# One core, block-sparse attention and a two-layer FFN: the same operations and transfers in another stored order, with 17 instead of 14 matmuls on zeros ahead of the first keys

## The chip, the cores and the metric

The kernel runs on one core of one Trainium2 chip. The engines named below are TensorE (PE), VectorE (DVE), ScalarE (ACT), GpSimd (POOL) and SyncE (SP, which here only issues transfers). The metric is the device time of one execution in microseconds. Before the change it is 259.52 us, the median of three runs (258.18 to 260.66).

## The reference

Inputs are q, k and v of 4 batches, 8 heads, 768 tokens and 64 columns, and the weights w_in (512 x 2048) and w_out (2048 x 512). Each head's keys are cut into 12 blocks of 64. A query attends to its own block and to the three blocks with the best gate scores, causally:

```python
k_rep = k.reshape(B, H, n_blocks, block, D).mean(axis=3)
gate_scores = np.einsum('bhsd,bhnd->bhsn', q, k_rep)
gate_scores = np.where(causal, gate_scores, -1000000000.0)
top_idx = np.argsort(gate_scores, axis=-1)[..., -top_k:]
...
scores = scale * np.matmul(q, k.transpose(0, 1, 3, 2))
mask = mask & (pos[:, None] >= pos[None, :])
scores = np.where(mask, scores, -1000000000.0)
attn = softmax(scores)
out = np.matmul(attn, v)
...
x = out.transpose(0, 2, 1, 3).reshape(B * S, H * D)
h = x @ w_in
g = 0.5 * h * (1.0 + np.tanh(c * (h + 0.044715 * h * h * h)))
return (g @ w_out).astype(np.float32)
```

(The softmax is written out in the reference; it is shortened here.) The 3072 tokens are the four batches one after the other, so the FFN of one batch needs all eight heads of that batch and nothing of the next.

## The kernel before

The work is cut into 16 pairs of heads, four pairs to a batch. A pair of the first batch goes through these steps, each on the engine named.

- SP (and for part of pair 0 ACT's queue) loads q, k and v of the pair (L392, L426). PE transposes q and k in float32, three 128 x 128 tiles at a time (`turn`, L548); ACT and DVE copy the results out (L361, L365).
- DVE sums the keys of each block (`ksb_h`, L583 and L589), PE multiplies q with these sums (the gate, L687), and DVE turns the result into a mask: a transpose (L703), the causal gate (L710), the eight largest of twelve (L719), and two steps that make the additive mask (L720, L724). PE transposes the mask (L756).
- PE computes the scores with the mask as part of the contraction (`st_e`, L863), ACT the exponentials (L882), POOL the causal triangle (an affine_select, L908). POOL also casts v (L363). PE multiplies with v (L931), DVE divides by the row sums (L949, L950), and PE transposes the output (L988).

The later batches have the same steps at other lines: q and k are transposed on DVE (L564) and cast (`kc_all`, `q16`: L363 on POOL, L361 on ACT or L365 on DVE), scores at L1046, exponentials at L1059, triangle at L1073, the product with v at L1085, the division at L969.

The FFN of a batch follows its attention and is interleaved with the attention of the next batch. `s1` (L1122) is x times w_in with the gelu on ACT (L1134). The second product of the first batch is plain (`s2_plain`, L1322). The later batches use a Strassen-like scheme with seven products instead of eight: `w_sums` (L1291) prepares sums of w_out on DVE, `sums` (L1309) sums of the activations on DVE, L1372 are the products, and the joins (L1421) add the parts on DVE. The last batch does a part of the first product in the same manner (L1170, L1211, L1235). Stores are issued at L1456 and L1465.

The weights are loaded by POOL (`load_w`): a small copy (L456) that waits for an earlier transfer, and then two transfers of a half each (L460). For w_in the copy waits for v of pair 2. SP has a transfer of its own that reads w_in (L1567) and waits until w_in is there; the loads of pair 4 (k, then q, then v) stand behind it on SP's queue. For w_out the copy waits for q of pair 4. So the order of the transfers is w_in, then k and q of pair 4, then w_out.

`warm` adds matmuls on zeros (L1524, 128 x 128 weights, 256 columns; "fillers" below). They depend on nothing and nothing reads them; each is executed where the order has it.

The order of everything is stored. All operations are first collected in a list with their numbers; `ORDER` gives the order in which they are emitted, `BUFFER` which buffer of a group each operation takes, and `ENGINE` which of the possible engines does an operation that more than one can do:

```python
for n in ORDER:
    op = self.ops[n]
    for kind, key in op.takes:
        if key not in self.buf:
            self.buf[key] = self.kinds[kind][0][next(picks)]
    op.emit(engine.get(n, next(iter(op.engines))))
```

Each engine works its own operations off in this order, and waits for others by semaphores. So of the one stored order only the order on each engine, and on each queue, is seen on the chip. Numbers that the text below speaks of: 71 and 62, 66 are the first transposes of pair 0 (q; k's first and second half), 75 its first gate, 157 the load of w_in, 172 that of w_out, 236 an affine_select of pair 1, 393 the first matmul of the FFN, 1890 to 1961 the fillers.

Of the kernel before, what the change touches and what calls it, by code (L numbers as in the profile page):

```python
# [21 lines left out]
    0, 22, 1890, 1891, 9, 1892, 1893, 1894, 6, 2, 1895, 1896, 1897, 1898,  # L22
    1899, 1900, 1901, 1, 1902, 12, 1903, 71, 1904, 15, 23, 1905, 1906, 1907,
    1908, 1909, 3, 1910, 72, 18, 1911, 62, 1912, 5, 1913, 82, 19, 1914, 195,
    1915, 31, 66, 64, 68, 73, 63, 74, 1916, 75, 1917, 100, 1918, 76, 1919,
    1920, 78, 77, 32, 67, 101, 35, 1921, 84, 93, 85, 89, 194, 83, 200, 79,
    4, 36, 80, 44, 1922, 1923, 98, 94, 1924, 196, 1925, 99, 1926, 201, 95,
    86, 91, 1927, 87, 113, 102, 90, 214, 114, 215, 103, 205, 104, 1928, 118,
    120, 202, 219, 26, 197, 206, 27, 119, 1929, 106, 210, 45, 52, 39, 115,
    40, 109, 107, 53, 121, 30, 111, 48, 1930, 1931, 129, 49, 220, 130, 198,  # L30
    203, 1932, 105, 207, 211, 122, 234, 131, 110, 249, 208, 123, 216, 235,
    1933, 1934, 57, 125, 133, 58, 250, 124, 240, 212, 224, 217, 221, 241,
    1935, 43, 157, 126, 127, 153, 134, 229, 254, 236, 222, 140, 225, 255,
    1936, 1937, 141, 138, 230, 242, 245, 155, 151, 231, 268, 238, 243, 149,
    232, 246, 237, 139, 269, 145, 1938, 279, 135, 142, 251, 263, 1939, 258,
    247, 1940, 280, 252, 264, 143, 270, 56, 1941, 144, 274, 283, 256, 275,
    259, 1942, 1943, 163, 1944, 284, 146, 276, 272, 147, 164, 226, 277, 285,
    288, 289, 227, 313, 281, 1945, 61, 297, 314, 165, 286, 1946, 302, 265,
    266, 290, 298, 271, 299, 308, 292, 168, 260, 303, 169, 300, 304, 309,
    293, 1947, 317, 322, 305, 310, 294, 306, 311, 261, 323, 315, 326, 318,  # L40
    393, 295, 328, 394, 329, 356, 395, 363, 1948, 396, 364, 1949, 319, 320,
    397, 365, 366, 324, 172, 367, 403, 404, 405, 178, 406, 358, 359, 327,
    360, 179, 330, 407, 361, 428, 429, 430, 335, 1950, 331, 362, 431, 336,
    339, 418, 419, 341, 432, 420, 421, 182, 398, 399, 1951, 400, 422, 401,
    408, 409, 410, 411, 402, 388, 183, 412, 389, 342, 390, 186, 391, 352,
    353, 392, 354, 355, 338, 383, 384, 385, 386, 343, 357, 344, 337, 413,
    387, 414, 415, 187, 347, 631, 349, 433, 416, 368, 434, 435, 369, 370,
    417, 346, 584, 1952, 436, 585, 373, 437, 371, 374, 345, 372, 632, 375,
    438, 376, 587, 378, 377, 439, 588, 379, 380, 348, 423, 440, 441, 442,
    424, 425, 426, 381, 443, 586, 444, 445, 427, 446, 447, 382, 448, 553,  # L50
    451, 635, 452, 453, 454, 449, 455, 574, 456, 457, 458, 575, 590, 459,
    460, 461, 566, 462, 567, 636, 1953, 463, 557, 464, 465, 466, 558, 470,
    552, 471, 472, 595, 473, 474, 475, 554, 476, 570, 190, 568, 477, 334,
    467, 591, 478, 692, 592, 571, 593, 555, 1954, 594, 479, 576, 1955, 693,
    191, 561, 480, 644, 559, 645, 481, 482, 483, 484, 572, 647, 485, 488,
    569, 696, 596, 489, 573, 562, 490, 486, 598, 491, 577, 697, 648, 622,
    556, 597, 560, 623, 563, 614, 639, 650, 578, 615, 492, 493, 564, 651,
    652, 654, 609, 640, 610, 494, 653, 495, 624, 957, 958, 601, 602, 496,
    497, 498, 605, 499, 705, 606, 655, 500, 656, 618, 658, 565, 646, 611,
    706, 603, 583, 501, 502, 709, 1956, 619, 616, 503, 507, 607, 657, 961,  # L60
    674, 508, 620, 711, 1957, 617, 682, 621, 625, 626, 509, 504, 510, 643,
    604, 511, 608, 512, 612, 683, 675, 665, 666, 712, 715, 678, 613, 713,
    513, 514, 627, 679, 700, 708, 628, 661, 716, 707, 515, 516, 714, 676,
    669, 677, 579, 517, 970, 518, 717, 662, 663, 580, 519, 670, 520, 667,
    664, 718, 521, 668, 680, 962, 719, 701, 726, 971, 974, 684, 671, 722,
    727, 681, 1020, 976, 704, 522, 672, 685, 1021, 728, 525, 686, 723, 739,
    526, 527, 735, 977, 673, 1024, 740, 528, 730, 741, 736, 529, 1025, 978,
    1958, 724, 737, 530, 1148, 731, 531, 743, 725, 468, 732, 729, 1033,
    1034, 532, 744, 733, 1037, 687, 738, 742, 533, 745, 756, 534, 980, 746,
    734, 840, 1039, 535, 747, 536, 981, 979, 1144, 758, 1040, 537, 748, 841,  # L70
    749, 972, 538, 450, 759, 1086, 1041, 1042, 544, 1145, 760, 761, 973,
    539, 545, 762, 540, 842, 1959, 843, 1082, 546, 768, 844, 769, 770, 1157,
    771, 1036, 1083, 830, 772, 1035, 831, 832, 833, 752, 1160, 1158, 1087,
    753, 754, 834, 755, 757, 1149, 763, 764, 765, 1095, 766, 825, 1096, 541,
    505, 1099, 767, 826, 548, 1101, 827, 773, 982, 828, 1161, 829, 782, 783,
    1045, 784, 1473, 523, 785, 792, 793, 786, 547, 794, 795, 835, 836, 837,
    1098, 1163, 1410, 796, 838, 774, 839, 811, 812, 984, 813, 814, 1102,
    1164, 787, 788, 1044, 789, 542, 815, 790, 777, 1043, 791, 845, 778, 779,
    780, 801, 487, 1028, 781, 1103, 802, 1104, 803, 804, 806, 985, 805, 807,
    808, 549, 809, 965, 816, 1165, 797, 817, 1105, 798, 818, 819, 810, 849,  # L80
    850, 851, 820, 1960, 1006, 852, 989, 966, 853, 1166, 846, 821, 775, 997,
    1048, 969, 854, 1414, 822, 855, 856, 857, 1535, 1007, 859, 860, 998,
    858, 861, 1097, 1029, 1477, 799, 823, 862, 1107, 863, 1002, 864, 865,
    1411, 847, 1090, 1008, 550, 1478, 1003, 1032, 993, 999, 866, 868, 1047,
    988, 1152, 994, 551, 990, 1004, 869, 870, 1010, 1005, 995, 1153, 800,
    1011, 871, 776, 1169, 991, 867, 872, 824, 1159, 1064, 1065, 1536, 1009,
    873, 1055, 1056, 874, 992, 996, 1059, 1060, 1000, 875, 1072, 877, 1073,
    878, 879, 1109, 848, 1012, 1068, 876, 1066, 1069, 1013, 1113, 880, 1001,
    885, 1014, 1114, 1156, 886, 887, 881, 888, 1110, 1423, 1070, 1106, 1067,
    1091, 1074, 524, 1474, 1051, 1415, 1015, 1071, 1075, 889, 890, 891, 892,  # L90
    895, 1061, 1418, 1052, 1115, 896, 1053, 1117, 897, 1118, 893, 1167, 898,
    1054, 1539, 894, 882, 899, 900, 901, 1492, 1076, 902, 1171, 904, 1597,
    1119, 1601, 1168, 905, 1172, 1094, 1121, 906, 907, 1130, 903, 908, 909,
# [1533 lines left out]
```

## Time and profile before

| what | value |
|---|---|
| times of the runs | 258.18, 259.52, 260.66 us |
| the profiled execution's own time | 259.66 us |
| its span, and what lies around it | 257.9 us, 1.76 us |
| PE busy | 249.0 us, 97% |
| DVE busy | 193.0 us, 75% |
| ACT busy | 180.6 us, 70% |
| POOL busy | 85.8 us, 33% |
| fillers (L1524) | 72 |
| TensorE clock shown as granted | 1.00 throughout |

In the rows of the profile, "L1122 PE MATMUL wide<-xT,w_in" is line 1122 on PE, writing the tile `wide` from `xT` and `w_in`. In the timeline the first two numbers are start and duration in microseconds, rows of one kind are merged ("x14"), and what ended the engine's idle time before stands in brackets. In the chain of waits the numbers are start and duration too. In the table by stretches come, after the stretch and its length, the busy time of PE, of PE's weight loads, of DVE, ACT and POOL (engines without work are left out), the granted clock, the share of the transfer engines and GB/s. In lists of waits come the total, the number and the longest, in microseconds.

### The profile page before, as it was taken

The page shows a single profiled execution, that of the slowest core. Times are in us where ns is not written, and L with a number is a line of the kernel's source. Part 1 is how long each engine was busy: PE and PEld are TensorE (multiplying, and loading weights), DVE is VectorE, ACT ScalarE, POOL GpSimd, SP SyncE. Part 2 cuts the span into 40 slices and gives each one's busy share as a digit, 9 for nine tenths or more (in the row PEclk, how much of TensorE's full clock was granted, in tenths as well). Part 3 has the DMA queues.
Part 4 walks back from the last instruction along what each step waited for, and adds up shares of the span by engine and source line. Part 5 has one row for each costly group of instructions (what it writes and reads, how often), then busy time and mean ns, then how long its engine had stood idle before and what let it go on. Part 6 is the DMA issues. An engine that isn't in the chain of part 4 may idle for free.

```text
span 257.9 us, 6488 instructions
## 1 busy us (share of the span) xinstructions
PE 249.0 (97%) x2506; PEld 172.8 (67%) x2506; DVE 193.0 (75%) x537; ACT 180.6 (70%) x228; POOL 85.8 (33%) x167
## 2 busy tenths in 40 slices
PE   6999999999999999999998999999999999999994
PEld 4767777655556665665776888556778787666883
DVE  1698955345248999998999987999797765678843
ACT  2487897655889999677987787566899857558200
POOL 8557551401045746120382445001184610000000
PEclk9999999999999999999999999999999999999999
DMA  7999969999999996999959948329131340120024
GB/s 151 221 220 169 218 114 145 145 185 179 145 146 139 134 151 133 140 204 193 140 107 177 198 117 137 64 44 265 25 56 47 61 82 34 41 84 0 4 81 163
DMA packets 130927, 32.62 MB, mean 126 GB/s; under 512 B 124528, under 2 KB 126928, under 8 KB 130896
## 3 DMA queue, kind: packets, MB, share of 16 engines
q1 hardware_dynamic: 126160, 27.62, 59.3%
q0 software_dynamic: 3136, 4.19, 10.0%
q10 hardware_dynamic: 1600, 0.39, 0.8%
q8 instruction: 19, 0.31, 0.5%
q14 instruction: 12, 0.10, 0.1%
HBM read 27.26 MB, written 6.29 MB: 130 GB/s over the span
## 4 chain that ended last, share of the span: by engine, by line
PE 80%; DVE 13%; ACT 2%; DMA 2%; issue 1%; POOL 0%; ACTq 0%; DVEq 0%
PE wide L1122 24%; PE bank L1372 18%; PE wide L1046 9%; PE bank L1322 8%; PE bank L1085 5%; PE wide L1211 5%; DVE XS L1309 2%; PE wide L863 2%; DVE sel L719 2%; PE bank L687 2%; PE bank L1524 2%; PE bank L931 2%; DMA G<-in_q_dram 2%; DVE sel L710 1%; PE bank L548 1%; PE bank L988 1%
## 5 line engine op out<-in xcount | busy, mean ns | idle before, releaser
L1122 PE MATMUL wide<-xT,w_in 128*128 128x384 f16 x416 | 73.7, 326 | 0.0
L1059 ACT ACTIVATE ats<-wide 128x896 f16<-128x896 f32 x72 | 63.6, 916 | 9.2 <-PE wide L1046 6.8
L1134 ACT ACTIVATE G<-wide 128x768 f16<-128x768 f32 x52 | 42.0, 809 | 25.6 <-PE wide L1122 25.5
L1122 PEld LDWEIGHTS <-w_in 128*128 128x128 f16 x416 | 39.8, 98 | 25.3 <-issue 1.0
L1073 POOL TENSOR_SCALAR_AFFINE_SELECT ats<-ats 128x256 f16<-128x256 f16 x72 | 32.0, 457 | 54.0 <-ACT ats L1059 50.0
L1046 PE MATMUL wide<-qT,kT 76*128 76x512 f16 (+3 forms) x192 | 38.9, 305 | 0.0
L1372 PE MATMUL bank<-w_out,G 128*128 128x256 f16 x216 | 32.2, 272 | 0.9 <-DVE osb L1421 0.9
L1372 PEld LDWEIGHTS <-G 128*128 128x128 f16 x288 | 27.0, 97 | 7.6 <-issue 1.2
L1322 PE MATMUL bank<-w_out,G 128*128 128x512 f16 x96 | 28.1, 379 | 0.0
L1421 DVE TENSOR_TENSOR osb<-bank,osb 128x512 f32<-128x512 f32 (+1 forms) x38 | 22.3, 594 | 7.2 <-PE bank L1372 4.4
L1085 PEld LDWEIGHTS <-ats 128*128 128x128 f16 x504 | 22.6, 98 | 5.8 <-POOL ats L1073 1.0
L564 DVE STREAM_TRANSPOSE s<-sd 128x768 f32<-128x768 f32 x24 | 23.1, 968 | 3.8 <-DMA sd<-in_q_dram 3.4
L1085 PE MATMUL bank<-v,ats 128*128 128x65 f16 x504 | 24.7, 194 | 0.3 <-POOL ats L1073 0.3
L882 ACT ACTIVATE ats<-wide 128x1024 f16<-128x1024 f32 (+3 forms) x24 | 20.9, 918 | 4.5 <-PE wide L863 4.3
L1046 PEld LDWEIGHTS <-kT 76*128 76x128 f16 x192 | 17.3, 98 | 10.0 <-issue 0.5
L363 POOL CAST kT<-s 64x768 f16<-64x768 f32 x20 | 17.3, 865 | 20.1 <-DVE s L564 19.7
L1372 PEld LDWEIGHTS <-XS 128*128 128x128 f16 x216 | 19.8, 98 | 4.5 <-DVE XS L1309 0.4
L1372 PE MATMUL bank<-TS,XS 128*128 128x256 f16 x144 | 22.6, 272 | 0.1
L363 POOL CAST v<-vsd 128x768 f16<-128x768 f32 x13 | 11.3, 870 | 26.9 <-DMA vsd<-in_v_dram 26.9
L1524 PE MATMUL bank<-XS 128*128 128x256 f16 x72 | 17.1, 326 | 1.1 <-DVE ks L302 1.1
L703 DVE STREAM_TRANSPOSE sel<-bank 128x160 f32<-128x160 f32 (+2 forms) x17 | 5.5, 330 | 14.7 <-PE bank L687 14.5
L969 DVE TENSOR_TENSOR xn<-bank,zr 128x384 f16<-128x384 f32 x24 | 13.4, 557 | 0.8
(116 smaller groups left out, 373.8 us busy)
## 6 DMA issues: line engine op xcount, KB each, us to landing
out_dram<-osb SPq DMA_DIRECT2D x23, 256.0 KB
vsd<-in_v_dram SPq DMA_DIRECT2D x26, 192.0 KB
sd<-in_k_dram SPq DMA_DIRECT2D x48, 96.0 KB
sd<-in_q_dram SPq DMA_DIRECT2D x48, 96.0 KB
w_in<-in_moe_w_in_dram POOLq DMA_DIRECT2D x2, 1024.0 KB, 11.3
w_out<-in_moe_w_out_dram POOLq DMA_DIRECT2D x2, 1024.0 KB, 12.8
G<-in_k_dram SPq DMA_DIRECT2D x6, 192.0 KB
TS<-in_v_dram SPq DMA_DIRECT2D x6, 192.0 KB
```

Of the source, the lines that this page charges most:

```text
L363: nc.gpsimd.tensor_copy(out=out, in_=in_)
L564: nc.vector.transpose(out=T[key + "T32", p], in_=T[key, p].rearrange("p t j -> p (t j)"))
L1046: nc.tensor.matmul(st[:, x:e], kT16[i][h][0:76, s0:s0 + 128], qT16[i][h][0:76, s0 + (x - cb):s0 + (e - cb)], start=True, stop=True)
L1059: nc.scalar.activation(out=T["at", u][:, 0:n], in_=plan.buf[("st",) + u][:, 0:n], func=AF.Exp, bias=0.0, scale=SCALE)
L1073: nc.gpsimd.affine_select(out=dg, in_=dg, compare_op=ALU.is_ge, fill=0.0, base=0, pattern=[[0, 2], [1, 128]], channel_multiplier=-1)
L1085: nc.tensor.matmul(pvv[:, qc, 0:65], at[:, cb + (qc - jc) * 128: cb + (qc - jc + 1) * 128], v16[i][:, jc, h, :], start=(gi == 0 and jc == ...
L1122: nc.tensor.matmul(hps[:, 512 * e:512 * e + HALF], w_in16[:, ci, (2 * j + e) * 128: (2 * j + e + 1) * 128], T["xT", b][:, ci, HALF * h:HAL ...
L1134: nc.scalar.activation(out=G[:, :, h, j, :], in_=plan.buf["hps", b, j, h].rearrange("p (e w) -> p e w", e=2)[:, :, 0:HALF], func=AF.Gelu_a ...
L1322: nc.tensor.matmul(plan.buf["ops", b, ti], G[:, f % 2, 2 * ti // NC, f // 2, ti % (NC // 2) * 128:ti % (NC // 2) * 128 + 128], w_out16[:, ...
L1372: nc.tensor.matmul(dst[:, HD * h:HD * h + HD], FACT[m][0][:, j, t * 128:(t + 1) * 128], FACT[m][1][:, j, :], start=(clear and j == 0), sto ...
L1421: nc.vector.tensor_tensor(out=dst(), in0=src(), in1=other(), op=ALU.add)
L1524: nc.tensor.matmul(plan.buf["warm", n][:, 0:256], zero16, z, start=True, stop=True)
```

## The change

The three tables are replaced; no other line changes. Operations and transfers are the same but for one filler that is left out (71 instead of 72). What is different on each engine:

- **PE**: 17 fillers stand ahead of the first transposes (operation 71) instead of 14, then 4 instead of 8 ahead of the next (62), 2 instead of 4 ahead of the third (66), and 2 instead of 1 between the fourth (73) and the first gate (75). Ahead of the first matmul of the FFN (393) stand 63 fillers instead of 58, behind it 8 instead of 14. The other matmuls are permuted locally.
- **POOL**: the load of w_in (157) comes behind the affine_select 236 instead of ahead of it, and ahead of a cast of v instead of behind it. A cast of k of pair 4 (337) comes ahead of w_out's load (172). The constants at the start are in another order.
- **SP**: the first ten transfers are the same; then v of pair 0 comes ahead of k of pair 3, and fills and some pairs of transfers change places.
- **DVE** and **ACT**: local permutations. Eleven operations go to DVE (nine from ACT, two from POOL) and eleven leave it (eight to ACT, three to POOL).

```diff
 ORDER = [
-    0, 22, 1890, 1891, 9, 1892, 1893, 1894, 6, 2, 1895, 1896, 1897, 1898,
-    1899, 1900, 1901, 1, 1902, 12, 1903, 71, 1904, 15, 23, 1905, 1906, 1907,
-    1908, 1909, 3, 1910, 72, 18, 1911, 62, 1912, 5, 1913, 82, 19, 1914, 195,
-    1915, 31, 66, 64, 68, 73, 63, 74, 1916, 75, 1917, 100, 1918, 76, 1919,
-    1920, 78, 77, 32, 67, 101, 35, 1921, 84, 93, 85, 89, 194, 83, 200, 79,
-    4, 36, 80, 44, 1922, 1923, 98, 94, 1924, 196, 1925, 99, 1926, 201, 95,
-    86, 91, 1927, 87, 113, 102, 90, 214, 114, 215, 103, 205, 104, 1928, 118,
-    120, 202, 219, 26, 197, 206, 27, 119, 1929, 106, 210, 45, 52, 39, 115,
-    40, 109, 107, 53, 121, 30, 111, 48, 1930, 1931, 129, 49, 220, 130, 198,
-    203, 1932, 105, 207, 211, 122, 234, 131, 110, 249, 208, 123, 216, 235,
-    1933, 1934, 57, 125, 133, 58, 250, 124, 240, 212, 224, 217, 221, 241,
-    1935, 43, 157, 126, 127, 153, 134, 229, 254, 236, 222, 140, 225, 255,
-    1936, 1937, 141, 138, 230, 242, 245, 155, 151, 231, 268, 238, 243, 149,
...
-    397, 365, 366, 324, 172, 367, 403, 404, 405, 178, 406, 358, 359, 327,
-    360, 179, 330, 407, 361, 428, 429, 430, 335, 1950, 331, 362, 431, 336,
-    339, 418, 419, 341, 432, 420, 421, 182, 398, 399, 1951, 400, 422, 401,
-    408, 409, 410, 411, 402, 388, 183, 412, 389, 342, 390, 186, 391, 352,
-    353, 392, 354, 355, 338, 383, 384, 385, 386, 343, 357, 344, 337, 413,
-    387, 414, 415, 187, 347, 631, 349, 433, 416, 368, 434, 435, 369, 370,
...
+    5, 3, 1890, 1891, 1892, 1893, 1894, 22, 1895, 9, 1896, 1897, 1898, 6,
+    1899, 1900, 12, 1901, 1902, 1903, 1904, 2, 1905, 1906, 71, 1907, 15,
+    1908, 1909, 23, 72, 1910, 62, 18, 82, 1911, 195, 1912, 64, 66, 73, 63,
+    1913, 1914, 75, 1915, 19, 74, 68, 0, 31, 100, 76, 78, 67, 77, 1916, 83,
+    1917, 1918, 1919, 1920, 84, 1921, 1, 32, 101, 93, 85, 79, 89, 35, 36,
+    194, 200, 80, 94, 4, 196, 26, 95, 1922, 1923, 1924, 91, 98, 86, 1925,
+    27, 1926, 99, 44, 1927, 87, 105, 113, 197, 102, 114, 115, 214, 45, 201,
+    205, 39, 1928, 90, 215, 103, 104, 118, 52, 202, 1929, 1930, 30, 53,
+    1931, 206, 1932, 207, 40, 120, 1933, 210, 219, 121, 1934, 106, 109,
+    1935, 211, 119, 107, 220, 129, 130, 198, 48, 234, 111, 110, 249, 131,
+    122, 49, 235, 203, 221, 208, 125, 1936, 212, 1937, 240, 123, 124, 250,
+    57, 224, 1938, 216, 217, 222, 133, 236, 126, 241, 254, 229, 127, 225,
+    58, 138, 157, 242, 139, 140, 255, 230, 245, 155, 43, 246, 268, 141, 238,
+    135, 243, 231, 251, 269, 1939, 232, 237, 258, 279, 56, 142, 263, 145,
+    280, 247, 143, 252, 1940, 144, 61, 1941, 264, 256, 274, 283, 270, 1942,
+    275, 151, 276, 1943, 134, 146, 265, 1944, 1945, 226, 272, 284, 277, 288,
...
+    356, 324, 329, 396, 364, 165, 327, 365, 366, 397, 1953, 330, 403, 404,
+    367, 405, 406, 358, 407, 359, 360, 335, 361, 428, 429, 331, 430, 362,
+    431, 168, 336, 418, 419, 169, 432, 337, 420, 421, 422, 172, 341, 339,
+    398, 399, 400, 401, 408, 342, 409, 410, 411, 402, 178, 345, 343, 388,
+    412, 389, 390, 1954, 1955, 391, 392, 352, 353, 354, 344, 355, 357, 179,
...
 ENGINE = {
     "ACT": [
-        63, 67, 72, 74, 85, 90, 94, 99, 101, 110, 119, 121, 331, 345, 348,
-        449, 467, 486, 504, 523, 541, 580, 594, 597, 598, 628, 654, 657,
-        658, 719, 749, 980, 981, 1043, 1044, 1105, 1106, 1167, 1168, 1202,
-        1382, 1433, 1434, 1620, 1668, 1674, 1677, 1698, 1704, 1707, 1727,
-        1733, 1736, 1822, 1858],
+        63, 67, 72, 74, 85, 90, 94, 99, 101, 110, 121, 130, 331, 346, 348,
+        349, 467, 486, 504, 523, 541, 580, 594, 598, 628, 655, 657, 658,
+        719, 749, 893, 929, 980, 981, 1043, 1044, 1105, 1106, 1167, 1202,
+        1346, 1382, 1558, 1620, 1668, 1674, 1677, 1698, 1704, 1707, 1727,
+        1733, 1736, 1822],
     "POOL": [
-        338, 587, 646, 647, 707, 708, 972, 973, 1035, 1036, 1097, 1098,
-        1159, 1160, 1425, 1426, 1488, 1489, 1551, 1612]}
+        337, 586, 587, 646, 647, 707, 708, 972, 973, 1035, 1036, 1097, 1098,
+        1159, 1160, 1426, 1488, 1489, 1551, 1612, 1613]}
```

272 rows, old and new, of tables (BUFFER, ORDER) are left out of this document.

## The prediction

> **What bounds the kernel now.** I read the totals first, then the shares of the chain of work that ended last, then what TensorE (PE) waited for, then busy time by stage.
>
> ```profile
> PE 249.0 (97%) x2506; PEld 172.8 (67%) x2506; DVE 193.0 (75%) x537; ACT 180.6 (70%) x228; POOL 85.8 (33%) x167
> PE 80%; DVE 13%; ACT 2%; DMA 2%; issue 1%; POOL 0%; ACTq 0%; DVEq 0%
> ```
> ```profile
> PE bank L548 <- DMA G<-in_q_dram: 1.2, 1, 1.2
> PE bank L1372 <- DVE osb L1421: 0.9, 1, 0.9
> PE bank L756 <- DVE madd L724: 0.8, 2, 0.5
> ```
> ```profile
> 0.00:5.50 5.50, 3.18 (x15) 1.99 (x15) 0.90 (x15) 1.28 (x1) 4.54 (x18) 1.00 0.73 143
> 41.00:80.00 39.00, 39.00 (x284) 22.31 (x283) 16.72 (x48) 27.27 (x37) 7.78 (x15) 1.00 1.12 163
> 80.00:130.00 50.00, 49.97 (x469) 31.13 (x468) 47.13 (x146) 42.89 (x55) 20.69 (x35) 1.00 0.95 151
> 130.00:140.00 10.00, 8.81 (x108) 6.62 (x105) 9.82 (x17) 8.12 (x11) 5.55 (x11) 1.00 0.72 151
> ```
>
> The reader is to see one engine, PE, that is nearly never idle. The program is the same work in another order, so it can gain in three ways only: fewer fillers (L1524, the matmuls on zeros) where PE has no wait to hide them in, the idle 1.2 us ahead of the first keys, and the waits on VectorE (DVE) at 11-33 and at 133-137 us. From 41 to 130 us PE is full (39.00 of 39.00, 49.97 of 50.00). There a filler costs its whole length and everything that arrives late is a new wait. DVE stands at 47.13 of 50.00 there and at 9.82 of 10.00 after it: the second engine is nearly a bound of its own.
>
> **The start, step by step.**
>
> ```profile
> 1.07 3.17 PE L1524 MATMUL bank<-XS 128*128 128x256 f16 x14 [1.07 <-DVE ks L302]
> 5.49 0.87 PE L548 MATMUL bank<-identk,G 128*128 128x128 f32 x3 [1.25 <-DMA G<-in_q_dram]
> 10.35 0.32 PE L687 MATMUL bank<-s,ksb 128*32 128x64 f32 x8
> ```
> ```profile
> 6.36 1.71 PE bank L1524 x8
> 8.07 0.64 PE bank L548 x3
> 8.71 0.85 PE bank L1524 x4
> 9.56 0.43 PE bank L548 x3
> 41.89 0.11 PE bank L1524
> ```
>
> A filler here costs 1.71 / 8 = 0.214 us; at 41.89 it costs 0.11. Three transposes cost 0.64, then 0.43. So PE runs at half speed until about 9.5 us, although the granted clock is shown as 1.00.
>
> Ahead of the first transposes 17 fillers stand in place of 14. The first transfers are the same, so the keys land when they did; 3 x 0.214 = 0.64 us goes into the wait of 1.25, and 0.6 us stays idle. That costs nothing and by itself gains nothing. Then 4 fillers stand in place of 8 and 2 in place of 4: the third group of transposes starts 6 x 0.214 = 1.28 us sooner, at 8.28 instead of 9.56. It and the group behind it then run at half speed (2 x (0.64 - 0.43) = 0.4 back), and one filler is added ahead of the first gate (0.2 at most). The gate at 10.35 moves by 1.28 - 0.4 - 0.2 = somewhat over 0.6 us.
>
> [...]
>
> ```profile
> 8.74 0.56 DVE L583 TENSOR_REDUCE ks<-bank 128x6 f32<-128x384 f32 x1 [1.09 <-PE bank L548]
> 55.11 0.54 DVE L365 CAST kT<-s 64x768 f16<-64x768 f32 x1
> ```
>
> Between that gate and the first FFN matmul (L1122, about 40 us) the new order has 7 more fillers, 0.77 us, mostly in holes that PE has there anyway while DVE finishes the masks (the 0.8 us of L756 is one part). On DVE a sum of block keys (L583, 0.56, and a short product) moves ahead of pair 1's gate, and a copy (L365, taken at 0.54) leaves the place ahead of pair 3's; these nearly cancel. ACT gives one copy and takes one. I take 0.5 us as the gain at the first FFN matmul. The ends are -0.2 (all new fillers on the path) and +1.2 (they hide, and the whole 1.28 stays).
>
> From there on 8 fillers stand in place of 14. Five of the six that go stood ahead of the 63 us mark: 5 x 0.11 = 0.54 us. So PE wants the second half of w_out 0.5 + 0.54 = 1.04 us sooner.
>
> **What is late next: w_out.**
>
> ```profile
> 22.18 0.20 POOL L456 COPY after_in<-TS 1x16 f32<-1x16 f32 x1
> 22.52 1.66 POOL L460 DMA_DIRECT2D w_in<-in_moe_w_in_dram  x2
> 24.24 0.63 POOL L908 TENSOR_SCALAR_AFFINE_SELECT ats<-ats 128x512 f16<-128x512 f16 x1
> ```
> ```profile
> 22.50 1.94 ACT L882 ACTIVATE ats<-wide 128x1024 f16<-128x1024 f32 x2 [0.95 <-PE wide L863]
> 18.97 0.45 PE L756 MATMUL bank<-ident,madd 128*128 128x128 f16 x5 [0.46 <-DVE madd L724]
> 21.82 0.28 PE L863 MATMUL wide<-XS,XS 64*128 64x256 f16 x2
> ```
> ```profile
> q0 software_dynamic: 1056, 2.10, 59.9%
> DMA  5959999992699999999999999999999300100049
> GB/s 119 249 122 230 238 277 240 176 119 27 78 176 213 210 221 212 230 204 246 207 223 209 224 207 242 204 225 229 201 201 180 62 12 8 33 0 0 0 71 152
> ```
> ```profile
> POOL after_out L456 <- DMA sd<-in_q_dram: 5.4, 1, 5.4
> ```
> ```profile
> 44.47 0.97 DVE L564 STREAM_TRANSPOSE s<-sd 128x768 f32<-128x768 f32 x1
> ```
> ```profile
> L363 POOL CAST kT<-s 64x768 f16<-64x768 f32 x20 | 17.3, 865 | 20.1 <-DVE s L564 19.7
> ```
> ```profile
> 37.23 0.57 SPq L1567 DMA_DIRECT2D after_in<-w_in  x1
> 46.92 1.78 POOL L460 DMA_DIRECT2D w_out<-in_moe_w_out_dram  x2 [0.22 <-issue]
> ```
> ```profile
> DMA to landing us min/median/max: 10.3/12.8/15.3
> ```
> ```profile
> 57.42 0.38 PE L1322 MATMUL bank<-w_out,G 128*128 128x512 f16 x1
> 63.26 0.81 PE L1322 MATMUL bank<-w_out,G 128*128 128x512 f16 x3
> ```
>
> w_out's two halves are issued by GpSimd (POOL) at 46.92 and 47.8 and land 10.3 and 15.3 us later, at 57.2 and 63.1. PE first uses them at 57.42 and with the second matmul of the 63.26 row, at 63.48. The slack is 0.2 and 0.35 us. PE cannot arrive sooner than that with any profit unless w_out lands sooner as well.
>
> It is tied to w_in: SP holds its queue until w_in has landed (37.23), loads k and q of pair 4 behind that, and POOL's copy of L456 waits for that q. And w_in's issue is moved: POOL now does the affine_select of 24.24 ahead of it. That one waits for the first exp of the 22.50 row, done at about 23.5. Unmoved, the issue would come at 23.5 + 0.63 + 0.34 = 24.5, 2.0 us late. But its score matmuls (21.82) stand closer behind pair 1's mask (18.97) than they did: some 1.4 us of PE work in between instead of 2.85. So the exp can end near 22.4 and w_in be issued at 23.4, 0.9 us late; with the 0.6 of the start it could be 0.3.
>
> Does a late issue reach the landing? The DMA rows (half-microsecond slices from 20 us on) dip to 27 and 78 GB/s at 24.5-25.5 and then carry about 210 GB/s to 35.5. 10 us x 210 GB/s = 2.1 MB, just w_in's queue (2.10). So w_in is the whole traffic from 25 on, and a late issue makes the dip longer. Between 0 (hidden in the 2 us from issue to first bytes) and 2.0 us I take 0.7, near the 0.9. w_out also has a cast of 0.87 us (L363, moved from DVE) ahead of it on POOL. It needs only k of pair 4, transposed on DVE at 44.47 to 45.44, and ends by 46.3, inside POOL's idle 5.4 us and ahead of w_out's own copy at about 46.5. I cost it at 0; that transpose later by 0.5 us would cost 0.3.
>
> With 0.7 the second half lands at 63.8. PE is there at 62.4, waits 1.4, and goes on 0.35 us later than before. One filler less follows (0.11). **Sum up to here: +0.24 us; the gain of the start is eaten whole.**
>
> **Behind 63 us** the counts of PE's work are equal. DVE gets 11 operations from ACT and POOL and gives 11 of much the same lengths to them.
>
> ```profile
> L1291 DVE TENSOR_TENSOR TS<-w_out x2: 683/683/683, 106.9 to 112.8; 128x1024 f16<-128x1024 f16 x2
> ```
> ```profile
> 132.71 1.20 DVE L1291 TENSOR_TENSOR TS<-w_out,TS 128x1024 f16<-128x1024 f16 x1
> 133.83 2.36 DVE L1309 TENSOR_TENSOR G<-G 128x768 f16<-128x768 f16 x2
> 136.12 0.68 DVE L1421 TENSOR_TENSOR osb<-bank,osb 128x512 f32<-128x512 f32 x1
> ```
>
> The wait of 0.9 at 136 is for the join of 136.12, which stood behind the two sums of 133.83. In the new order this join and the second of these sums come ahead of the weight sum of 132.71 and of the first, longer sum. The join is sooner, the weight sum 0.68 and about half a microsecond later, 1.2 in all, and PE has a like amount of score and value matmuls moved ahead of the matmul that reads it. I take these as even. The ends are a gain of 1.2 (PE's idle time of 130-140, 10.00 - 8.81, goes) and a loss of 1.2. Near 105 us a weight sum (L1291, 0.68) moves ahead of pair 9's selection, and between 140 and 180 us DVE takes over four copies (0.54 each) and gives three operations away, 0.54 net. PE's order leaves it other work at both; I take 0, ends 0 and +1.2. At the end a copy moves from ACT to DVE and one filler goes; nothing waits on either for long: 0.
>
> **Forecast: 259.66 + 0.24 = 259.9 us.** The profiled execution took 259.66 (span 257.9 and 1.76 around it), 0.14 above the median of the runs shown, 259.52; the three lie between 258.18 and 260.66, so about 1% is what a measurement can tell from no change.
>
> **Rivals.**
>
> *The clock opens early, or w_out keeps up.* The trace's clock opened at 9.5, after 4 us of unbroken work. 17 fillers are 17 x 0.214 + 0.2 = 3.85 us, nearly as long, so it may open at 5 to 6 us. The transposes and fillers up to 9.5 then cost half, about 1.4 us less; w_in is issued 0.9 - 1.4 = 0.5 us sooner than before, w_out lands at 62.6 and PE is 0.9 ahead: 259.66 - 0.85 - 0.11 = 258.7. If the idle 1.2 us at 130-140 goes too, 257.5. For it: the length of the filler row. Against it: 0.6 us of idle remain ahead of the keys, and the row of 8.71 shows half speed 3.2 us after work went on.
>
> *DVE becomes the bound* (slower). DVE works in order. If the 1.2 us at 132.71 comes on the path, and the 0.68 and 0.54 as well, PE waits 2.4 us more: 259.66 + 0.24 + 2.4 = 262.3. It decides once DVE's idle time there (2.87 us of 80-130, 0.18 of 130-140) is not where the new order needs it. For it: 47.13 of 50.00. Against it: PE's 1.4 us wait at 63 lets DVE catch up.
>
> *The change doesn't do what it says*: 17 fillers end at 4.92, the keys come at 5.49, and if w_in's issue were not late either (slack of 0.35 stays), 259.66 - 0.35 - 0.11 = 259.2.
>
> **How the numbers follow.** w_out eats the gain: 0.43 (259.2 to 261.2, from a w_in late by 0 to 2.0). Clock early or w_out in time: 0.23 (256.3 to 258.7). DVE the bound: 0.25 (261.1 to 263.6, the far end with w_in at its worst). Nothing: 0.09. Leaving out a tenth at either end gives 257.0 to 262.4. Under 256.9 (1% off the median) lies the far end of the second case, 0.15. Above 262.1 lies most of the third and what the first gives with small losses of the third beside it, 0.25. Within 1% is the rest, 0.60.
>
> **What would show it.** Right: the first gate at about 9.75; fillers at 0.21 us until about 9.5; w_in issued after 23 us; a new wait of PE on w_out at L1322 of about 1.4 us near 62 us. Wrong: fillers at 0.11 before 7 us; no wait at L1322; a wait of PE of over 2 us on L1291, L1309 or L1421 between 120 and 170 us; the end of PE's last row away from 254 us by more than 2.5.

## The result and the profile after

The changed kernel takes 257.19 us (median of ten runs, 256.44 to 258.20), the kernel before 258.56 us (median of ten, 258.18 to 260.66). The ratio is 0.9934, 95% interval 0.9908 to 0.9960: two thirds of a percent faster. The forecast was 259.9 us and no gain. The profiled execution took 257.58 us (span 255.9) against 259.66 (257.9). That of the kernel before lies 1.1 us above the median of its ten runs, that of the changed kernel 0.4 us above its own, so the traces differ by more than the medians do.

First the busy time by stretch of the changed kernel:

```profile
0.00:5.50 5.50, 3.88 (x18) 2.52 (x19) 1.01 (x15) 1.28 (x1) 4.45 (x22) 1.00 0.75 144
41.00:80.00 39.00, 37.47 (x252) 20.88 (x250) 16.41 (x47) 25.92 (x34) 8.80 (x15) 1.00 1.20 164
80.00:130.00 50.00, 49.88 (x480) 31.15 (x479) 46.63 (x147) 42.84 (x55) 21.25 (x35) 1.00 0.84 133
130.00:140.00 10.00, 10.00 (x126) 8.02 (x124) 9.72 (x20) 9.33 (x12) 4.83 (x9) 1.00 1.25 204
```

What PE waited for:

```profile
PE bank L1322 <- DMA w_out<-in_moe_w_out_dram: 1.5, 1, 1.5
PE bank L756 <- DVE madd L724: 0.7, 3, 0.3
PE bank L548 <- POOL cgate L480: 0.5, 1, 0.5
```

Two stretches have changed places. 41-80 us, full before, has lost 1.53 us, all of it in one wait on w_out. 130-140 us, where 1.19 us were missing, is full. The row of L548 names POOL. The transposes behind it start where they did (5.43 against 5.49 us), so I take it for the same wait for the first keys: it is 0.5 instead of 1.2 us.

The start in the timeline of the changed kernel:

```profile
1.07 3.81 PE L1524 MATMUL bank<-XS 128*128 128x256 f16 x17 [1.07 <-DVE ks L302]
5.43 0.87 PE L548 MATMUL bank<-identk,G 128*128 128x128 f32 x3 [0.55 <-POOL cgate L480]
6.09 1.06 PE L1524 MATMUL bank<-XS 128*128 128x256 f16 x4
6.95 0.57 PE L548 MATMUL bank<-identk,G 128*128 128x128 f32 x3
8.55 0.32 PE L687 MATMUL bank<-s,ksb 128*32 128x64 f32 x8
```

The gate comes at 8.55 instead of 10.35. Half speed ends at about 7 us (three transposes in 0.57 where they took 0.85) and not at 9.5. The prediction and the expectations call this the opening of the clock: the two traces show the lengths of PE's operations, and the granted clock as 1.00 before it and after it. The row of L1122 below (its first and last start stand behind the lengths) has the first FFN matmul at 38.9 instead of 40.3:

```profile
L1122 PE MATMUL wide<-xT,w_in x416: 323/326/337, 38.9 to 227.2; 128*128 128x384 f16 x139
```

Then the gain is gone, as the timeline shows:

```profile
22.27 1.66 POOL L460 DMA_DIRECT2D w_in<-in_moe_w_in_dram  x2
46.17 1.78 POOL L460 DMA_DIRECT2D w_out<-in_moe_w_out_dram  x2 [0.26 <-issue]
57.62 0.38 PE L1322 MATMUL bank<-w_out,G 128*128 128x512 f16 x1 [1.53 <-DMA w_out<-in_moe_w_out_dram]
63.24 0.81 PE L1322 MATMUL bank<-w_out,G 128*128 128x512 f16 x3
```

PE first uses w_out at 57.62, 0.2 us later than before, and stands at 63.24 where it stood at 63.26. Of 1.4 us nothing is left. The gain that stays is made behind that. On DVE, near 131 us:

```profile
131.15 0.69 DVE L1291 TENSOR_TENSOR w_out<-w_out 128x1024 f16<-128x1024 f16 x1
131.76 0.68 DVE L1421 TENSOR_TENSOR osb<-bank,osb 128x512 f32<-128x512 f32 x1
132.95 0.89 DVE L1291 TENSOR_TENSOR TS<-w_out,TS 128x1024 f16<-128x1024 f16 x1
133.76 1.23 DVE L1309 TENSOR_TENSOR G<-G 128x768 f16<-128x768 f16 x2
```

The weight sum that took 1.20 us takes 0.89, and two sums of activations take 1.23 instead of 2.36. That is the same work on the same shapes. The last join ends the chain at 252.02 + 0.69 instead of 254.09 + 0.69.

### The profile page after: what moved, and what is told of

It is laid out like the page before. It is cut to its first block, busy times and chain, and to the rows that moved or that the text cites. A ratio compares the mean times of both kernels' runs of the same rounds, so it can differ in the third digit from the quotient of the medians.

```text
span 255.9 us, 6491 instructions
## 1 busy us (share of the span) xinstructions
PE 247.5 (97%) x2505; PEld 172.2 (67%) x2505; DVE 191.0 (75%) x537; ACT 178.5 (70%) x227; POOL 87.8 (34%) x168
## 4 chain that ended last, share of the span: by engine, by line
PE 70%; SPq 12%; DVE 9%; DMA 2%; POOL 2%; issue 2%; ACT 2%; DVEq 0%; POOLq 0%; ACTq 0%
PE bank L1372 20%; PE wide L1122 18%; SPq L398 11%; PE wide L1046 10%; PE bank L1085 6%; PE wide L1211 5%; PE bank L1322 3%; DMA sd<-in_q_dram 2%; PE wide L863 2%; PE bank L687 2%; DVE ks L583 1%; DVE s L564 1%; DVE sel L719 1%; PE bank L931 1%; SPq L392 1%
## 5 line engine op out<-in xcount | busy, mean ns | idle before, releaser
L1122 PE MATMUL wide<-xT,w_in 128*128 128x384 f16 x416 | 74.2, 326 | 0.0
L1122 PEld LDWEIGHTS <-w_in 128*128 128x128 f16 x416 | 39.9, 98 | 27.3 <-issue 2.8
L1073 POOL TENSOR_SCALAR_AFFINE_SELECT ats<-ats 128x256 f16<-128x256 f16 x72 | 32.8, 471 | 69.0 <-ACT ats L1059 66.6
L1046 PE MATMUL wide<-qT,kT 76*128 76x512 f16 (+3 forms) x192 | 38.1, 305 | 0.0
L1372 PE MATMUL bank<-w_out,G 128*128 128x256 f16 x216 | 31.4, 272 | 0.0
L1322 PE MATMUL bank<-w_out,G 128*128 128x512 f16 x96 | 28.5, 379 | 1.5 <-DMA w_out<-in_moe_w_out_dram 1.5
L1085 PEld LDWEIGHTS <-ats 128*128 128x128 f16 x504 | 21.8, 98 | 4.6 <-POOL ats L1073 0.7
L1085 PE MATMUL bank<-v,ats 128*128 128x65 f16 x504 | 24.1, 194 | 0.0
L363 POOL CAST kT<-s 64x768 f16<-64x768 f32 x21 | 18.1, 865 | 16.9 <-DVE s L564 14.6
L363 POOL CAST v<-vsd 128x768 f16<-128x768 f32 x13 | 11.9, 916 | 15.9 <-DMA vsd<-in_v_dram 15.8
L1524 PE MATMUL bank<-XS 128*128 128x256 f16 x71 | 15.4, 317 | 1.1 <-DVE ks L302 1.1
L719 DVE MAX8 sel<-sel 128x8 f32<-128x12 f32 x160 | 13.2, 157 | 0.6
```

The source lines that it names most:

```text
L363: nc.gpsimd.tensor_copy(out=out, in_=in_)
L1046: nc.tensor.matmul(st[:, x:e], kT16[i][h][0:76, s0:s0 + 128], qT16[i][h][0:76, s0 + (x - cb):s0 + (e - cb)], start=True, stop=True)
L1073: nc.gpsimd.affine_select(out=dg, in_=dg, compare_op=ALU.is_ge, fill=0.0, base=0, pattern=[[0, 2], [1, 128]], channel_multiplier=-1)
L1085: nc.tensor.matmul(pvv[:, qc, 0:65], at[:, cb + (qc - jc) * 128: cb + (qc - jc + 1) * 128], v16[i][:, jc, h, :], start=(gi == 0 and jc == ...
L1122: nc.tensor.matmul(hps[:, 512 * e:512 * e + HALF], w_in16[:, ci, (2 * j + e) * 128: (2 * j + e + 1) * 128], T["xT", b][:, ci, HALF * h:HAL ...
L1322: nc.tensor.matmul(plan.buf["ops", b, ti], G[:, f % 2, 2 * ti // NC, f // 2, ti % (NC // 2) * 128:ti % (NC // 2) * 128 + 128], w_out16[:, ...
```

## The experiments

All tables are changed by hand from one of the two stored orders; nothing else is, but where it is said. The experiments' tables are written in fewer lines, so line numbers there are smaller by 5 (by 7 to 11 where many fillers are left out): L1317 is L1322 above. Each ratio is to the kernel before in runs on the same chip. That kernel's medians were 258.6 to 259.6 us in the five comparisons, so kernels of different comparisons are compared by their ratios. A ratio and its interval are not worked out from the two medians, and can differ from the ratio of the medians by a few tenths of a percent.

| kernel | median, us | ratio to the kernel before (95%) |
|---|---|---|
| the change | 257.19 | 0.9934 (0.9908 to 0.9960) |
| changed order, start 14, 8, 4 | 257.42 | 0.9932 (0.9904 to 0.9960) |
| old order, start 17, 4, 2 | 258.23 | 0.9999 (0.9960 to 1.0038) |
| changed order, w_out behind k | 255.80 | 0.9887 (0.9845 to 0.9928) |
| changed order, DVE's join late | 257.11 | 0.9927 (0.9897 to 0.9956) |
| old order, POOL's casts away | 257.82 | 0.9942 (0.9914 to 0.9970) |
| changed order, POOL's casts back | 258.58 | 0.9986 (0.9961 to 1.0012) |
| old order, a piece of PE's order | 259.07 | 0.9983 (0.9956 to 1.0009) |
| w_out behind k, no late fillers | 255.22 | 0.9840 (0.9802 to 0.9877) |
| old order, three edits | 255.14 | 0.9839 (0.9787 to 0.9892) |
| w_out behind k, start fillers only | 255.82 | 0.9836 (0.9792 to 0.9879) |
| three edits, start 17, 4, 2 | 255.92 | 0.9875 (0.9849 to 0.9901) |
| three edits, start 20, 1, 2 | 255.21 | 0.9840 (0.9813 to 0.9866) |

### Is the start worth anything?

The new order with the old start, and the old order with the new start:

```diff
 changed order, fillers ahead of operations 71, 62 and 66
-    17, 4, 2
+    14, 8, 4
 old order, fillers ahead of operations 71, 62 and 66
-    14, 8, 4
+    17, 4, 2
```

> The changed order with the fillers of the old start: 14, 8 and 4 ahead of the first three groups of transposes instead of 17, 4 and 2 (74 fillers in all), everything else as changed. Both theories: the clock opens later than the 6.95 us of the changed kernel's trace, and the first FFN matmul comes at 39.8 to 40.3 us instead of 38.87. Theory W (from 57 us on the landing of w_out sets the time, so the start has no part in the 1.4 us that the change gained): the wait of PE at L1322 shrinks from 1.5 to under 0.7 us and the time stays within 0.5 us of the changed kernel's 257.2. Theory S (the gain is that of the start): 258.3 to 258.7 us.

> The old order with the fillers of the new start: 17, 4 and 2 instead of 14, 8 and 4 (69 in all), nothing else changed. Both theories: the first FFN matmul about 1.0 to 1.4 us sooner than 40.26. Theory W: a new wait on w_out at L1322 of about 1 us, the second half first used between 63.1 and 63.5, and a time 0 to 0.35 us under that of the old order (258.2 to 258.6). Theory S: 1.0 to 1.4 us faster, 257.2 to 257.6.

Measured: 0.9932, the change's own ratio, with the old start: theory S falls here. With the new start alone it is 0.9999, no gain that can be told, but the interval is wide (0.9960 to 1.0038). The median of that kernel is 0.9 us under the kernel before (258.23 against 259.13), and three of its twelve runs, above 261 us, undo that in the ratio. A gain of up to 0.4% is not excluded, which is where theory S begins. The trace of the first kernel holds a surprise, too (rows of the changed order with 14 fillers):

```profile
1.07 3.17 PE L1519 MATMUL bank<-XS 128*128 128x256 f16 x14 [1.07 <-DVE ks L297]
5.47 0.52 PE L543 MATMUL bank<-identk,G 128*128 128x128 f32 x3 [1.24 <-DMA G<-in_q_dram]
57.57 0.38 PE L1317 MATMUL bank<-w_out,G 128*128 128x512 f16 x1 [1.49 <-DMA w_out<-in_moe_w_out_dram]
```

I had expected the clock later and the wait under 0.7 us. The first transposes already take 0.52 instead of 0.87, after only 14 fillers and an idle time of 1.24 us; the first FFN matmul comes at 38.9 all the same, and the wait is again 1.5 us. So this execution had no later start, and against theory S stand only the times. In the old order with 17 fillers that matmul comes at 38.0, and the wait is new:

```profile
PE bank L1317 <- DMA w_out<-in_moe_w_out_dram: 1.3, 1, 1.3
```

The kernel before had none there. Of 2.3 us of start 1.3 us became waiting; w_out is first used at 56.5 instead of 57.4 us.

The same is seen where nothing of the start was changed. The kernel "old order, a piece of PE's order" (below) differs from the kernel before near 134 us alone. In its trace the clock was open at the first transposes all the same:

```profile
5.35 0.52 PE L543 MATMUL bank<-identk,G 128*128 128x128 f32 x3 [1.11 <-DMA G<-in_q_dram]
8.43 0.32 PE L682 MATMUL bank<-s,ksb 128*32 128x64 f32 x8
```
```profile
PE bank L1317 <- DMA w_out<-in_moe_w_out_dram: 1.0, 2, 0.7
```

The gate comes at 8.43, sooner than in the changed kernel, and the first FFN matmul at 38.5, 1.8 us sooner than in the trace of the kernel before. PE then waits 1.0 us for w_out, and the first matmul on its second half comes at 63.09 instead of 63.48. So an early start in a trace need not come from the count of fillers, and w_out's landing takes most of it in the old order too.

### Is it w_out's landing that caps it?

```diff
-load_w(..., prio, ("v", 2) if x == "in" else prev)
+load_w(..., prio, ("v", 2) if x == "in" else ("k", HP))
 ORDER: operation 172 (w_out's load) directly behind 165 (k of pair 4)
```

> The changed order, but w_out's load waits for k of pair 4 instead of q of pair 4, and stands on GpSimd ahead of the cast of k of pair 4. It is issued at about 42 instead of 46.17 us. Theory W: it lands 1.5 to 3 us sooner, the wait of 1.5 us at L1322 goes, and the time falls by 1.0 to 1.5 us to about 256. Rival: q of pair 4 and the loads behind it share the transfer engines with it, w_out lands hardly sooner or the gate of pair 4 becomes the wait: no gain, 257.0 to 257.5.

Measured: 255.80 us, 0.9887 against the change's 0.9934. It was issued at 43.3, not 42, and that was enough (the stretch and the issue, of this kernel):

```profile
41.00:64.00 23.00, 23.00 (x151) 13.47 (x150) 8.75 (x24) 14.39 (x19) 3.71 (x5) 1.00 1.27 176
```
```profile
L455 POOL DMA_DIRECT2D w_out<-in_moe_w_out_dram x2: 881/892/902, 43.3 to 44.2; - x2
```

PE is full from 41 to 64 us; the wait of 1.53 is gone, and by the ratios 1.2 us come out in the time. The cap is shown. The intervals of the two ratios overlap a little (0.9845 to 0.9928 and 0.9908 to 0.9960), so its size is less sure.

### What filled PE at 130-140 us?

The forecast had two candidates, the join's place on DVE and PE's own order. Each was tried, the first by undoing it in the new order, the second alone in the old one.

```diff
 changed order, DVE: the join (867) and a sum (776)
-    867 776 551 800
+    551 800 776 867
 old order, PE: two products (874, 875) behind score and value matmuls
-    873 1055 874 992 996 1059 1000 875 1072 877
+    873 1055 992 996 1059 1000 1072 874 875 877
```

> The changed order with one piece undone on DVE: the join and the sum that the change put ahead of the weight sum (L1291) and the long sum (L1309) near 131 us stand behind that long sum again; PE keeps the changed order. Theory J (this order on DVE is what took the 1.2 us of idle time out of 130-140): a wait of PE on the join (L1421) of about 1 us comes back and the time is 0.8 to 1.5 us longer, 258.0 to 258.7. Rival (PE's own new order, with score and value matmuls moved ahead, did it): within 0.4 us of 257.2.

> The old order with one piece of PE's new order alone: the two products that read the last weight sum (third and fourth of their group) stand behind the score and value matmuls of 134 to 135.4 us instead of among them. Theory Q: PE no longer waits 0.5 us at 133 us, and the wait for the join at 136 stays, since nothing of DVE is changed; 0.3 to 0.6 us faster if that wait doesn't grow, or no change where the 0.5 us only moves to the join. Theory P: no change, the idle time of 130-140 stays near 1.2 us.

Measured: 0.9927, nothing lost with the join late; so theory J falls. And 0.9983 for the piece of PE's order: no change, so theory Q, in as much as this piece stands for it, falls too. In that trace the wait for the weight sum has moved into the wait for the join:

```profile
PE bank L1367 <- DVE osb L1416: 1.2, 1, 1.2
```

What was left were the lengths on DVE. In the old order three casts of POOL lie in the stretch where DVE works off its sums (timeline of the kernel before):

```profile
128.85 0.82 POOL L363 CAST v<-vsd 128x768 f16<-128x768 f32 x1
132.47 0.90 POOL L363 CAST kT<-s 64x768 f16<-64x768 f32 x1
134.50 0.82 POOL L363 CAST v<-vsd 128x768 f16<-128x768 f32 x1
```

The new order has none of them between 122 and 139 us. I had read POOL's order only around the two weight loads. So this one edit was made in the old order, and undone in the new:

```diff
 old order, POOL: cast v 9 (1032), cast k 11 (1159), cast v 11 (1156)
-    969 1097 1008 1032 999 1004 995 991 1159 1012 1066 1156 1070
+    969 1097 1032 1008 999 1004 995 991 1012 1066 1070 ... 1159 1156
 changed order, POOL
-    1032 969 999 1008 1004 991 995 1012 1066 ... 1156 1159
+    969 1032 999 1008 1004 991 995 1159 1012 1066 1156 ...
```

> The old order with only GpSimd's order changed: its casts of k and v of pairs 9 and 11 (L363), which stood among the affine_selects of 128 to 136 us, come ahead of that stretch (v of pair 9) or behind it, near 140 us. Theory P (these casts lengthen DVE's sums of L1291 and L1309, which took 0.89, 1.20 and 1.90 us in the trace against 0.69, 0.89 and 0.67 in the changed kernel, and that made PE's idle 1.2 us of 130-140): the sums take under 0.95 us, PE is idle under 0.4 us in that stretch, and the time falls by 0.8 to 1.4 us. Theory Q (PE's own new order covers the wait for DVE): the idle time stays near 1.2 us and the time within 0.4 us of the old order's.

> The changed order with GpSimd's three casts put back among the affine_selects where the old order had them. Theory P: the sums of L1291 and L1309 near 131 to 135 us take 1.2 to 1.9 us again, PE becomes idle by 0.5 to 1.2 us in 130-140, and the time is 0.5 to 1.2 us above the changed kernel's 257.2. Theory Q: PE stays full in 130-140 even where the sums get longer, and the time stays within 0.4 us.

Measured: 0.9942 and 0.9986. Taking the casts out of the old order gives 1.1 us in the medians of that comparison, nearly the whole gain of the change. The edit of the new order brought only two of the three back into the stretch: there the cast of v of pair 9 stands behind another cast of v, and in the trace both ran at 120.0 to 121.7 us. These two already take most of the gain away (1.3 us, by the ratios; the interval includes no gain at all). Theory P holds both ways, and so do its lengths. Old order without the casts:

```profile
129.83 0.68 DVE L1286 TENSOR_TENSOR w_out<-w_out 128x1024 f16<-128x1024 f16 x1
130.99 0.78 DVE L1286 TENSOR_TENSOR TS<-w_out,TS 128x1024 f16<-128x1024 f16 x1
131.69 1.43 DVE L1304 TENSOR_TENSOR G<-G 128x768 f16<-128x768 f16 x2
```
```profile
130.00:140.00 10.00, 10.00 (x131) 8.12 (x129) 9.46 (x18) 9.04 (x11) 5.66 (x11) 1.00 0.65 128
```

New order with the two casts, in the timeline first DVE, then POOL, and the stretch:

```profile
130.84 0.69 DVE L1286 TENSOR_TENSOR w_out<-w_out 128x1024 f16<-128x1024 f16 x1
132.51 1.31 DVE L1286 TENSOR_TENSOR TS<-w_out,TS 128x1024 f16<-128x1024 f16 x1
133.74 2.21 DVE L1304 TENSOR_TENSOR G<-G 128x768 f16<-128x768 f16 x2
```
```profile
132.12 1.16 POOL L358 CAST kT<-s 64x768 f16<-64x768 f32 x1
133.23 1.53 POOL L1068 TENSOR_SCALAR_AFFINE_SELECT ats<-ats 128x256 f16<-128x256 f16 x2
134.72 0.82 POOL L358 CAST v<-vsd 128x768 f16<-128x768 f32 x1
```
```profile
130.00:140.00 10.00, 9.09 (x108) 6.66 (x106) 9.77 (x17) 8.15 (x10) 6.14 (x11) 1.00 1.21 191
```

The sum of 131.15 in the changed kernel meets no POOL operation (POOL is idle from 130.95 to 131.85 us there) and takes 0.69. The one at 132.51 in the new order with the two casts meets the cast that runs until 133.28 and takes 1.31: it ends at 133.82, 0.54 us behind the cast's end, as if nearly all of it came after. Against the changed kernel's rows (0.89 and 1.23) this sum and the two behind it are longer by 1.4 us together, and PE, full without the casts, is idle for 0.91 us. The affine_selects seem to do the like on a smaller scale, but not always: the sum of 0.89 in the changed kernel, at 132.95, starts while three of them run, until 133.30; that of 129.83 in the old order without the casts takes 0.68 beside two of them (129.82 to 131.21).

So the rows show the lengths, 0.62 us more on a sum of 0.69; by what means the cast lengthens the sum they do not show. Whether the casts' own lengths (a cast of k takes 0.82 us in the median of twenty in the kernel before, and 1.16 in this trace) grow from the same cause no run here tells apart.

### Can both kernels be beaten?

With w_out early, PE is never idle between 41 and 64 us, so the fillers behind the first FFN matmul should cost their length.

```diff
 changed order, w_out behind k, ORDER behind operation 393
-    8 fillers
+    none
```

> The changed order with w_out's load behind k of pair 4 (as in the run with that one change) and, besides, without the 8 fillers behind the first FFN matmul. PE is never idle between 41 and 130 us in that run, so by theory W each of the 8 costs its 0.107 us: 0.86 us less than the 255.8 us of that run, about 254.9. Rival: the fillers stand where PE would wait for DVE or for w_out anyway, or they keep the clock up: no gain, 255.6 to 256.2.

Measured: 255.22 us, 0.9840 against 0.9887. The medians differ by 0.6 us and the ratios by 1.2, where 0.86 was expected. Part of the gain becomes a wait: in 140-250 us PE is busy for 109.10 instead of 109.64 of 110 us.

Then the same causes in the old order, whose DVE, PE and engine tables stay as they were:

```diff
 old order
+    POOL's three casts out of 128-136 us
+    w_out's load waits for k of pair 4
-    14 fillers behind operation 393
```

> The old order and the old engine choices with three edits: GpSimd's casts of pairs 9 and 11 out of 128-136 us (as in the run with that edit alone, 257.8 us), w_out's load waiting for k instead of q of pair 4, and the 14 fillers behind the first FFN matmul left out. By theories W and P the new order as such is worth little beside these causes: the casts give 1.1 us, the 14 fillers 14 x 0.107 = 1.5 us, since with w_out early nothing caps PE, and the time falls to 255.0 to 256.2. Rival (the rest of the searched order, on DVE and PE, carries a good part of the gain): 256.8 to 258, with new waits of PE behind 64 us.

Measured: 255.14 us, 0.9839. Three edits to the old order reach what the new order reaches with two. It is the fastest median of the study, 1.6% under the kernel before, and level with the new order's 255.22. The rest of the searched order carries nothing that these runs can see, which is about half a percent.

The last three kernels ask what the fillers at the start do once nothing caps PE.

```diff
 changed order, w_out behind k, no late fillers
-    38 fillers between the first gate and the first FFN matmul
 old order, three edits, ahead of operations 71, 62 and 66
-    14, 8, 4
+    17, 4, 2     (one kernel)
+    20, 1, 2     (another)
```

> The run without late fillers (255.2 us) also without the 38 fillers between the first gate and the first FFN matmul; the 25 ahead of that gate stay. Theory F (in this stretch PE waits for DVE's masks anyway, and the fillers only fill those waits): the idle time of 10-39 us grows by 2 to 4 us, the first FFN matmul comes 0 to 1 us sooner than 38.7, and the time is 254.2 to 255.2. Rival (the fillers keep the clock up): matmuls at half speed somewhere in 10-39 us, the first FFN matmul later, 255.5 to 258.

> The old order with the three edits (255.14 us, runs from 254.79 to 257.05) and, besides, the start of the change: 17, 4 and 2 fillers instead of 14, 8 and 4. Nothing caps PE at 57 us any more, so what the start is worth must show in the time. Theory C (when the clock opens varies from one execution to the next, whatever the count; the fewer fillers behind the first transposes save time only where it opens late): the median within 0.5 us of 255.1, and a largest time nearer to the median than 1.9 us. Rival (17 fillers open the clock sooner by a fixed amount): 0.8 to 1.4 us faster, 253.7 to 254.3.

> The same with 20, 1 and 2 fillers: at half speed 20 fillers reach until 5.35 us, so that PE has no idle time left ahead of the first keys. Theory C: as with 17, median 254.6 to 255.6, the clock of the profiled execution open somewhere between 4.5 and 8 us. Rival (unbroken work from 1.07 us on opens the clock after a fixed time): the first transposes take 0.33 to 0.35 us in the trace instead of 0.65, and the time is 0.5 to 1.2 us under that with 17.

Measured: 0.9836 without the 38 fillers, against 0.9840 with them: no difference that can be told, though the median of 255.82 lies above what theory F expected. They fill holes. PE's busy time in 10-39 us falls from 28.49 to 25.59, which is the idle time that theory F asks for; the first FFN matmul came at 39.0, no sooner, in an execution whose clock was late:

```profile
1.07 3.81 PE L1513 MATMUL bank<-XS 128*128 128x256 f16 x17 [1.07 <-DVE ks L291]
7.16 0.85 PE L537 MATMUL bank<-identk,G 128*128 128x128 f32 x3
```

In 10-39 us a matmul takes 0.056 us there on average (25.59 us, 456 of them) and 0.058 with the fillers (28.49 us, 488 of them), so the rival's half speed without these fillers is not seen over that stretch as a whole; a short piece of it would not show in this mean.

With 14, 17 and 20 fillers the ratios are 0.9839, 0.9875 and 0.9840. There is no order in that. The median with 17 is 0.8 us above that with 14, not below; its trace has a wait of 0.48 us for k of pair 3 at 18.9 us and an FFN that starts at 38.8 instead of 37.8. The one with 20 has its first transposes at full speed (0.52 us) and is 0.7 us under the one with 17, both as the rival had it; it is level with the one with 14, which a fixed effect of the count does not give. What the start's fillers are worth stays open within about half a percent; a gain of 0.8 us from 17 of them is not there.

## Why the prediction was wrong

**The start: too small, and the excess belongs to the execution.** The idle time ahead of the keys fell to 0.55 (0.6 forecast), and the gate came 1.80 us sooner where somewhat over 0.6 was taken. The first FFN matmul gained 1.4 us against 0.5; the end of the range was +1.2. The term that was mis-sized is the clock: it opened at 7 instead of 9.5 us, the first half of the first rival. But that is not shown to be the work of the 17 fillers: with 14 fillers the old order had its gate at 8.43 and the first FFN matmul at 38.5 in another trace. The sum took the clock of one execution for that of the kernel.

**What is late next: right, its size by luck.** PE had a new wait on w_out, 1.53 us where 1.4 was forecast, and it stood at 63.24 against 63.26 us. The sum up to there, +0.24, was -0.02 in the trace. It came together in another way than I had it. Of the fillers that go I put five ahead of the 63 us mark (0.54 us); the traces have five there before and three after, so two go, 0.21 us. w_in was issued at 22.27, not at 23.4, since the exponentials ahead of it began at 20.34 instead of 22.50 us; how much of that is the clock's is not shown. The 2 us from issue to first bytes, in which w_in's delay could have been hidden, are 1.6 to 1.7 us in the trace of the kernel before (issued at 22.52, the first packets of its queue at 24.15 to 24.2). w_out was issued 0.75 us earlier than before, and took longer, 16.1 us at the most where it was 15.3. And the wait was at the first half, not at the second. I had written of the first half's slack (0.2 us) and then reckoned with the second's. That the wait came out within 0.1 us of the forecast is luck. The changed order with DVE's join late is the same up to here and issued w_out at 46.1 us too; in its trace PE waited 0.5 us, for the second half:

```profile
62.19 0.81 PE L1317 MATMUL bank<-w_out,G 128*128 128x512 f16 x3 [0.49 <-DMA w_out<-in_moe_w_out_dram]
```

That a late w_out takes most of an earlier start is seen in the traces of two kernels in the old order, and that w_out's issue is the reason is shown by the kernel with w_out behind k.

**Behind 63 us: this step failed.** "I take these as even" put 0 on 130-140 us, with a gain of 1.2 as one end. The trace took the end: 1.19 us of idle time went, and the products of 136.85 came at 135.33, 1.5 us sooner (kernel before, changed kernel):

```profile
136.85 0.86 PE L1372 MATMUL bank<-w_out,G 128*128 128x256 f16 x6 [0.90 <-DVE osb L1421]
135.33 0.82 PE L1372 MATMUL bank<-w_out,G 128*128 128x256 f16 x6
```

I had looked for the cause in the order of DVE and of PE and weighed the one against the other. Both were tried and neither does it: with the join late nothing is lost, and the piece of PE's order that was tried gives nothing. The cause is on POOL, an engine that no wait of PE named. Its three casts are moved out of the stretch, and DVE's sums are no longer lengthened by them. I took durations as constants from rows (1.20, 2.36) that held this very contention; the lengths of one form in the trace of before would have warned me (shortest, median and longest, in ns):

```profile
L1291 DVE TENSOR_TENSOR TS<-w_out,TS x4: 683/692/1195, 107.7 to 132.7; 128x1024 f16<-128x1024 f16 x4
```

**DVE as the bound: not seen.** No wait of over 2 us appeared; 80-130 us stays full (49.88 of 50.00). The moved weight sum near 105 us and the copies of 140-180 us cost nothing, as taken.

**The sum.** -0.02 up to 63 us, about -1.5 by 137 us, and the rest later: the last join starts 2.07 us sooner. Where this last half microsecond comes from stays open. The first rival with the idle time of 130-140 gone was put at 257.5 us, and the profiled execution took 257.58. But that price had the right total by the wrong terms: 0.85 us of it was to come from a w_out 0.5 us early, and none did. The ten runs' median lies in the range given (257.0 to 262.4); the direction of the forecast is wrong. Its base, 259.66, was one execution, 1.1 us above the median of ten (258.56).

## What to carry to other kernels

Where one engine is full for 90 us, ask of a gain ahead of it which transfer it runs into; if the slack there is 0.2 us, the gain is 0.2 us, and the transfer's trigger is the edit to make. Read the order of every engine in the stretch that waits, also of the one that nothing waits for: where two operations of one line and shape differ in length in the timeline, look at what runs beside the longer one. And when a new search moves many operations, find the few edits that carry its gain: here one of them, three casts moved in the old order, gave nearly all of it, and with two edits that the search had not made (w_out's trigger, and all late fillers left out) the old order gained more than twice as much.

## What the runs showed of the hardware

When the clock opens (PE goes over from 0.214 to 0.107 us a filler) varies between these traces and does not follow the count of fillers. With 14 fillers the first transposes ran at full speed (0.52 us) in three of five traces, two of them quoted above, after 3.17 us of work and 1.1 to 1.2 us of idle time; in the other two, the kernel before among them, half speed lasted beyond 8.4 us. With 17 it was open ahead of the transposes in four of eight traces, and in that of the kernel with the start fillers only three transposes still took 0.85 us at 7.16. The earliest is the changed order with w_out behind k:

```profile
1.07 3.39 PE L1519 MATMUL bank<-XS 128*128 128x256 f16 x17 [1.07 <-DVE ks L297]
```

Its 17 fillers took 3.39 instead of 3.81 us. That is 0.42 us less, four fillers at 0.107 us instead of 0.214, so by this estimate full speed began at 3.9 us, after 2.8 us of work. The opening then lies anywhere between 3.9 and 9.5 us in these traces. The length of the work alone does not give it: in the trace of the changed order with 14 fillers the first transposes were at full speed at 5.47, where PE had worked 3.17 us and been idle for 1.24 since, and in that of the kernel before the same 3.17 us and an idle 1.25 left them at half speed (0.87 us at 5.49). What sets it no run here shows.

Beside a cast on POOL, a weight sum of DVE (128 x 1024) took 1.31 us instead of 0.69. I had not expected a POOL operation of 0.8 us to cost PE time, two engines further on.
